# Chunked attention feeding a gated MLP on one core: the order of the SyncE queue, the staging of loads, and the casts of the opening

## The chip, the core and the metric

One NeuronCore of a Trainium2 chip. The time of a run is the device time of the program in microseconds. The kernels were run on several chips, so each is compared only with runs of the kernel before on the same chip. A run within 1.5% of the fastest of its kernel counts as fast.

## The reference, cut to what matters

```python
# q, k, v: 8 batches, 8 heads, 576 tokens, 64 columns; chunks of 64 tokens
scores = scale * np.matmul(q_c, k_c.transpose(0, 1, 2, 4, 3))
attn = softmax(scores)
x = np.matmul(attn, v_c) ...            # as 4608 tokens x 512
h = x @ w_in                            # 512 -> 2048
g = h * (1.0 / (1.0 + np.exp(-beta * h)))
out = g @ w_out                         # 2048 -> 512
```

Nearly all the arithmetic is in the two products with w_in and w_out. Attention is within chunks of 64 tokens and small.

## The kernel before

The tokens go through in nine blocks of 512: block b is the first 512 tokens of batch b, and block 8 collects the last 64 of each batch. For each block TensorE runs mm1 (x by w_in, 64 matmuls of 128x512, read from xT) and mm2 (g by w_out, 64 matmuls); the attention of the *next* block (scores, exp, attend, normalize) is strewn into mm2. So TensorE has always work, if the next block's xT is there when mm2 ends.

xT is x turned so that the 512 columns stand on partitions. From block 1 on this is done by DMA transposes; q and k are turned likewise from block 2 on (block 0 and 1 turn q and k on TensorE). All these transposes and all loads are issued by one engine, SyncE, in the order in which they stand; it waits for the data of the first in the queue before it looks at the second (a wait of 18.1 us of this kind is shown below). Stores are issued by ScalarE.

```python
def load(blk, name, m):                       # a quarter of q, k or v: 256 KB
    ...
    P.dma("sp", lambda e: e.dma_start(stage[name][r:r + n, 512 * m:512 * m + 512]..., drams[name]...),
          writes=[K(name + "stage", m, r, v=blk)])

def turn_qk(blk, name):                       # cast q or k of a whole block, turned
    P.dma("sp", lambda e: e.dma_start_transpose(turned[name]..., cast[name][:, :]), ...)

def turn_x(blk, m):                           # a quarter of x, turned
    P.dma("sp", lambda e: e.dma_start_transpose(xT[:, blk % 2, :, 128 * m:...], x_sb[:, m, :]), ...)
```

Every operation is given a time in an ideal schedule of 32 units a block, and `at(time, ...)` sorts them; this order is the order of each engine's queue. T is the moment at which mm2 of the block before starts.

```python
def attention(blk, T):
    # scores at T + 0.6, exp at T + 1 ...
    for u in range(2):
        for m in (2 * u, 2 * u + 1):
            at(T + 4.6 + 4 * u, attend, blk, m)
            at(T + 4.7 + 4 * u, normalize, blk, m)
            at(T + 4.8 + 4 * u, turn_x, blk, m)

def prepare(blk, T):
    for i, name in enumerate("qkv"):
        for m in range(4):
            at(T - 27 + 4 * i + m, load, blk, name, m)
            if name == "v":
                at(T - 8 + m, cast_v, blk, m, "pool")
            else:
                at(T - 14 + 4 * i + m, cast_qk, blk, name, m, "pool")
                if m == 3:
                    at(T - 10 + 4 * i, turn_qk, blk, name)
```

A block is 32 units, so the load of q for the next block, at T - 27, is at T + 5 of this one: between the turns of x at T + 4.8 and at T + 8.8. The loads have one staging buffer for each of q, k and v, and in the opening w_out is loaded into the staging of w_in:

```python
wstage = sb("wstage", [128, 4, 2048], F32)      # w_in pieces, then w_out pieces, in the same four slots
stage = {n: sb(n + "stage", [128, 2048], F32) for n in "qkv"}
...
at(-87.9, load_beta)      # the load on SyncE, and the halving of beta on VectorE right behind it
at(-80 + u, cast_qk4, 0, "q", u, "dve")         # later in VectorE's queue than beta
at(-0.5, cast_w_in, 1, 1, ("dve",))             # frees a slot of wstage
at(0, load_w_out, 0)
```

The softmax here doesn't subtract the row's maximum and nothing guards it: scores larger than these inputs give would overflow.

## Time and profile before

| what | kernel before |
|---|---|
| time | 358.55 us (median of 4, 355.67 to 360.55) |
| span of the profiled run | 354.5 us |
| TensorE busy | 293.9 us, 83% of the span |
| mm1 waits for xT | 25.1 us in 6 waits, and 4.3 more put down to "issue" |
| mm1 of block 1 starts at | 77.67 us |

The lines of the profile name the engines PE (TensorE's matmuls), PEld (its weight loads), DVE (VectorE), ACT (ScalarE), POOL (GpSimd), SP (SyncE) and SPq (SyncE's DMA queue); L399 is line 399 of the kernel, out<-in are the tiles written and read, and a bracket at the end of a line is the idle time before it in us, with what ended it. The clock is the share of full speed that was granted to TensorE.

These rows of the page give the busy share of TensorE and of the DMA engines in 40 slices of 8.9 us each, in tenths:

```profile
PE   0047998729996999799979995999499959999995
DMA  7980999998059946993899199908992499732013
```

TensorE has a dip (6, 7, 7, 5, 4, 5) about once in each four slices: the block boundaries. The DMA row has a 0 at the fourth slice, which the window of that stretch shows closer (length, busy time and count of PE, PEld, DVE, ACT, POOL, then clock, DMA share, GB/s), and SyncE's own waits give what the queue stood at:

```profile
26.30:35.40 9.10, 6.35 (x139) 5.05 (x140) 6.08 (x12) 3.70 (x7) 1.04 (x1) 1.00 0.01 2
```

```profile
SPq L267 <- DVE w_in_bf L259: 22.0, 3, 18.1
```

L267 is the load of w_out; it waited 22.0 us in three waits, the longest 18.1, for VectorE to empty the shared slots. And the copy of a turned k of block 0, on the timeline (start, us, engine, line, what):

```profile
25.15 2.43 DVE L259 COPY kT<-F 128x1024 bf16<-128x1024 bf16 x1 [1.38 <-PE F L327]
```

### The profile page before, as it was taken

How to read it: one execution, taken by the hardware profiler on the slowest of the kernel's cores; microseconds unless marked ns; L12 is line 12 of the kernel's file. 1: busy time of each engine (PE TensorE's matmuls, PEld its weight loads, DVE VectorE, ACT ScalarE, POOL GpSimd, SP SyncE). 2: the span in 40 equal slices, each digit the busy share in tenths (PEclk: the TensorE clock that was granted, in tenths of full speed). 3: DMA queues.
4: the chain of work that ended last, by engine and by line, in shares of the span. 5: the costliest groups of instructions: out<-in, count | busy, mean ns of one | idle time of the engine just before them, and what ended most of it. 6: DMA issues, size and time to landing. Idle time of an engine off the chain costs nothing.

```text
span 354.5 us, 5695 instructions
## 1 busy us (share of the span) xinstructions
PE 293.9 (83%) x2384; PEld 137.9 (39%) x2384; DVE 149.6 (42%) x237; ACT 153.5 (43%) x228; POOL 73.6 (21%) x112
## 2 busy tenths in 40 slices
PE   0047998729996999799979995999499959999995
PEld 0035444304442444244424441444144424444442
DVE  0166896306630653074317410743066306633810
ACT  1053777206711771176127512761167116715721
POOL 2321447411003400340034013300340024100000
PEclk9999999958998999899989996999789989999999
DMA  7980999998059946993899199908992499732013
GB/s 248 252 329 2 305 399 212 226 226 118 2 124 243 198 92 143 250 199 64 179 251 208 46 199 212 213 2 182 216 217 41 124 213 183 134 100 79 0 39 82
DMA packets 156665, 58.06 MB, mean 164 GB/s; under 512 B 144352, under 2 KB 149472, under 8 KB 156640
## 3 DMA queue, kind: packets, MB, share of 16 engines
q1 hardware_dynamic: 151392, 48.26, 66.3%
q10 hardware_dynamic: 5248, 9.44, 9.1%
q8 instruction: 19, 0.31, 0.4%
q14 instruction: 6, 0.05, 0.1%
HBM read 36.71 MB, written 9.44 MB: 130 GB/s over the span
## 4 chain that ended last, share of the span: by engine, by line
PE 62%; SPq 17%; DMA 9%; DVE 8%; issue 2%; ACT 1%
PE F L399 39%; PE F L414 18%; SPq L283 10%; DMA xT<-x_sb 8%; SPq L381 6%; DVE x_sb L375 3%; DVE kT L259 3%; PE A L348 2%; PE A L365 2%; DMA beta_raw<-in_moe_beta_dram 1%; PE F L327 1%; DVE qcast L259 1%; DVE rden L373 1%; SPq L311 1%; PE F L389 1%
## 5 line engine op out<-in xcount | busy, mean ns | idle before, releaser
L399 PE MATMUL F<-xT,w_in_bf 128*128 128x512 bf16 x576 | 139.8, 408 | 29.9 <-DMA xT<-x_sb 25.1
L407 DVE SCALAR_TENSOR_TENSOR g<-tt,F 128x512 bf16<-128x512 bf16 x144 | 98.5, 687 | 111.9 <-ACT tt L404 111.6
L414 PE MATMUL F<-w_out_bf,g 128*128 128x512 bf16 x576 | 130.3, 379 | 0.0
L404 ACT ACTIVATE tt<-F,beta_half 128x512 bf16<-128x512 f32 x144 | 99.0, 687 | 71.8 <-PE F L399 71.8
L399 PEld LDWEIGHTS F<-xT,w_in_bf 128*128 128x128 bf16 x576 | 59.1, 104 | 110.2 <-issue 51.1
L414 PEld LDWEIGHTS F<-w_out_bf,g 128*128 128x128 bf16 x576 | 54.3, 98 | 62.8
L419 ACT ACTIVATE ostage<-F 128x512 f32<-128x512 f32 x36 | 21.5, 597 | 93.9 <-PE F L414 93.9
L259 POOL CAST qcast<-qstage 128x512 bf16<-128x512 f32 x28 | 17.2, 614 | 134.1 <-DMA qstage<-in_q_dram 134.1
L373 DVE RECIPROCAL rden<-A 128x8 f32<-128x8 f32 x36 | 7.3, 203 | 55.2 <-PE A L365 55.2
L259 POOL CAST vaug<-vstage 128x512 bf16<-128x512 f32 x36 | 22.3, 619 | 35.8 <-DMA vstage<-in_v_dram 35.8
L259 POOL CAST kcast<-kstage 128x512 bf16<-128x512 f32 (+1 forms) x31 | 20.3, 655 | 35.7 <-DMA kstage<-in_k_dram 35.7
L375 DVE TENSOR_TENSOR x_sb<-A,rden 128x512 bf16<-128x512 f32 x36 | 24.9, 692 | 1.2
L354 ACT ACTIVATE E<-A 128x512 bf16<-128x512 f32 x36 | 18.7, 602 | 7.0 <-PE A L348 7.0
L327 PE MATMUL F<-identity,qcast 128*128 128x128 bf16 x16 | 2.0, 308 | 21.4 <-DVE qcast L259 21.4
L365 PEld LDWEIGHTS A<-vaug,E 64*64 64x64 bf16 x576 | 11.7, 112 | 8.4 <-issue 4.3
L365 PE MATMUL A<-vaug,E 64*64 64x65 bf16 x576 | 14.2, 198 | 0.9 <-ACT E L354 0.4
L256 ACT ACTIVATE qT<-F 128x1024 bf16<-128x1024 bf16 x2 | 4.9, 2442 | 19.6 <-PE F L327 19.6
L261 POOL TENSOR_SCALAR w_out_bf<-wstage 128x512 bf16<-128x512 f32 (+1 forms) x5 | 9.5, 1910 | 15.2 <-DMA wstage<-in_moe_w_out_dram 15.2
L348 PE MATMUL A<-qT,kT 64*64 64x64 bf16 x576 | 7.4, 199 | 4.0 <-DVE kT L259 3.9
L327 PEld LDWEIGHTS F<-identity,qcast 128*128 128x128 bf16 x16 | 1.5, 138 | 21.6 <-POOL w_in_bf L259 18.0
L348 PEld LDWEIGHTS A<-qT,kT 64*64 64x64 bf16 x576 | 6.1, 112 | 7.9 <-DVE kT L259 4.6
L228 DVE TENSOR_SCALAR beta_half<-beta_raw 128x16 f32<-128x16 f32 x1 | 0.9, 893 | 16.4 <-DMA beta_raw<-in_moe_beta_dram 16.4
(29 smaller groups left out, 48.2 us busy)
## 6 DMA issues: line engine op xcount, KB each, us to landing
vstage<-in_v_dram SPq DMA_DIRECT2D x32, 256.0 KB, 5.2
out_dram<-ostage ACTq DMA_DIRECT2D x32, 256.0 KB, 2.9
qstage<-in_q_dram SPq DMA_DIRECT2D x24, 256.0 KB, 5.1
kstage<-in_k_dram SPq DMA_DIRECT2D x24, 256.0 KB, 5.2
wstage<-in_moe_w_out_dram SPq DMA_DIRECT2D x4, 1024.0 KB, 10.5
wstage<-in_moe_w_in_dram SPq DMA_DIRECT2D x3, 1024.0 KB, 9.5
qstage<-in_q_dram SPq DMA_DIRECT2D x4, 512.0 KB, 6.1
kstage<-in_k_dram SPq DMA_DIRECT2D x4, 512.0 KB, 7.2
```

Of the source, the lines that this page charges most:

```text
L259: P.op(eng, lambda e: e.tensor_copy(dst, src), reads=r, writes=wr)
L283: return e.dma_start(stage[name][r:r + n, 512 * m:512 * m + 512].rearrange("p (h d) -> p h d", d=64), drams[name][b, :, t:t + n, :].rearra ...
L348: return e.matmul(A[64 * c2:64 * c2 + 64, bank, col:col + 64], turned["k"][r, hp, t], turned["q"][r, hp, t])
L354: P.op("act", lambda e: e.activation(E[:, bank, :], A[:, bank, :], AF.Exp, scale=0.125), reads=[K("A", bank, v=("s", blk))], writes=[K("E" ...
L365: return e.matmul(A[r, bank, 128 * (h % 4):128 * (h % 4) + 65], E[r, 2 * (m // 2) + h % 2, col:col + 64], vaug[r, m, h, 0:65])
L375: P.op("dve", lambda e: e.tensor_tensor(x_sb[:, m, :].rearrange("p (b h d) -> p b h d", h=4, b=2), o[:, :, :, 0:64], rden[:, m, :, :].unsq ...
L381: P.dma("sp", lambda e: e.dma_start_transpose(xT[:, blk % 2, :, 128 * m:128 * m + 128], x_sb[:, m, :]), reads=[K("x", m, v=blk)], writes=[ ...
L399: P.op("pe", lambda e, c=c: e.matmul(F[:, bank, :], w_in_bf[:, c, 256 * e0 + i:256 * e0 + 256:2], xT[:, blk % 2, c, :], start=(c == 0), st ...
L404: P.op("act", lambda e: e.activation(tt[:, T % NTT, :], F[:, bank, :], AF.Tanh, scale=beta_half[:, e0, i:i + 1]), reads=[K("F", bank, v=(" ...
L407: P.op("dve", lambda e: e.scalar_tensor_tensor(g2[:, t, :], tt[:, T % NTT, :], 1.0, F[:, bank, :], ALU.add, ALU.mult), reads=[K("F", bank, ...
L414: P.op("pe", lambda e, t=t: e.matmul(F[:, s, :], g2[:, t, 128 * s:128 * s + 128], w_out_bf[:, t, :], start=(t == 0), stop=(t == NT - 1)), ...
L419: P.op("act", lambda e: e.activation(ostage[:, N % NOS, :], F[:, s, :], AF.Copy), reads=[K("F", s, v=("o", N))], writes=[K("o", N % NOS, v ...
```

## The change

The intent has four parts. (1) Loads of blocks 3 to 8 stand so early that they run two blocks ahead, in doubled staging; in the SyncE queue of a period the four turns of x and the turns of the next q and k come first, the twelve loads last. (2) In the opening, q and k of block 0 are cast as they land, beta is halved later and by GpSimd. (3) w_out has its own staging, so its load waits for nothing. (4) Smaller things: turned q and k are written contiguously and read strided; x of block 1 is turned on TensorE; mm1 of block 0 starts with half the columns; three output stages instead of four, for room. The core of the diff:

```diff
-        wstage = sb("wstage", [128, 4, 2048], F32)
-        stage = {n: sb(n + "stage", [128, 2048], F32) for n in "qkv"}
+        wstage = sb("wstage", [128, 8, 2048], F32)
+        stages = {n: sb(n + "stage", [128, 2, 2048], F32) for n in "qkv"}
-        NOS = 4
+        NOS = 3
 ... (beta)
-            P.op("dve", lambda e: e.tensor_single_scalar(
+        def halve_beta():
+            P.op("pool", lambda e: e.tensor_single_scalar(
 ... (copies of turned q, k)
-            copy(eng, turned[name]....rearrange("x h (p i) -> x h i p", i=4),
-                 mid.rearrange("x (h i p) -> x h i p", h=2, i=4),
+            copy(eng, turned[name]....rearrange("x h (p i) -> x h p i", i=4),
+                 mid.rearrange("x (h i p) -> x h p i", h=2, i=4),
 ... (prepare)
-                    at(T - 27 + 4 * i + m, load, blk, name, m)
+                    at((T - 48 if blk > 3 else T - 42 if blk == 3 else T - 26) + 4 * i + m,
+                       load, blk, name, m)
                     if name == "v":
-                        at(T - 8 + m, cast_v, blk, m, "pool")
+                        at(T - (17 if blk > 2 else 9) + m, cast_v, blk, m, "pool")
                     else:
-                        at(T - 14 + 4 * i + m, cast_qk, blk, name, m, "pool")
+                        at(T - (41 if blk > 3 else 35 if blk == 3 else 22) + 4 * i + m,
+                           cast_qk, blk, name, m, "pool")
                         if m == 3:
-                            at(T - 10 + 4 * i, turn_qk, blk, name)
+                            at(T - (20 if blk > 2 else 12.5) + 2 * i, turn_qk, blk, name)
 ... (opening)
-            at(-80 + u, cast_qk4, 0, "q", u, "dve")
-            at(-80 + u, cast_qk4, 0, "k", u, "pool" if u == 0 else "dve")
-        at(0, load_w_out, 0)
-            at(4 * j + 0.6, load_w_out, j)
-            at(14, load, 1, "v", m)
+        at(-83, load_w_out, 0)
+            at(-61, load_w_out, j)
+            at(-60, load, 1, "v", m)
+            at(-79 + i, cast_qk4, 0, name, u, "dve")
+        at(-75, halve_beta)
 ... (x of block 1)
-                at(28.9 + 2 * u, turn_x, 1, m)
+            at(30.2 + 0.2 * m, turn_x_pe, 1, m, A, (0, 2, 1, 3)[m], ("act", "dve")[m % 2])
 ... (mm1 of block 0: columns 0 to 255 of its first four tiles first)
```

## The prediction

> **What bounds the kernel now.** I read the chain that ended last first, then the same chain in order of time, then windows, and at last the opening on a timeline. The chain by share, and the costliest group:
>
> ```profile
> PE 62%; SPq 17%; DMA 9%; DVE 8%; issue 2%; ACT 1%
> ...
> L399 PE MATMUL F<-xT,w_in_bf 128*128 128x512 bf16 x576 | 139.8, 408 | 29.9 <-DMA xT<-x_sb 25.1
> ```
>
> TensorE carries only 62% of the chain; 17% is time of SyncE's DMA queue (SPq) and 9% the flight of a transfer. The matmuls of the first product (mm1, L399) stood idle 29.9 us, nearly all for xT, the attention output turned by a DMA. In order of time, one block boundary (start us, us, what):
>
> ```profile
> 135.26 0.70 DVE x_sb L375
> ...
> 136.37 1.26 SPq L381
> ...
> 137.68 0.58 SPq L283
> 138.31 0.67 SPq L283
> 139.02 1.23 SPq L283
> 140.29 1.07 SPq L283
> ...
> 141.42 1.84 SPq L381
> ...
> 143.31 3.53 DMA xT<-x_sb
> ...
> 146.98 15.66 PE F L399 x64
> ```
>
> L283 is the load of q, k or v; L381 the turn of x. Four q loads of the next block stand in the queue between the second and the third turn of x, although x was ready: 3.7 us of issuing, and then the last turn flies 3.53 us behind loads. Windows (length, then busy time by engine, PEclk, DMA share, GB/s), the first two over a whole period of 128 matmuls of 512 columns, the second two over mm1 just after a wait and later:
>
> ```profile
> 128.67:162.64 33.97, 31.72 (x258) 14.43 (x256) 14.43 (x25) 15.45 (x24) 7.25 (x12) 0.95 0.82 171
> ...
> 306.61:336.60 29.99, 29.94 (x257) 14.08 (x256) 14.41 (x25) 15.45 (x24) 0.00 (x0) 1.00 0.19 55
> ...
> 146.90:150.70 3.80, 3.72 (x10) 0.55 1.15 269
> 150.70:162.60 11.90, 11.90 (x57) 1.00 0.98 193
> ```
>
> The last period has no loads behind it, and it is the model for the change: 29.99 us, TensorE busy for 29.94. The others take 34.73, 33.97, 33.95, 37.01, 37.39 and 35.62 us by the starts in the chain. Part is the wait, and part that after the wait the clock is at 0.55 for 3.8 us, which makes mm1 15.66 instead of 13.81 us.
>
> Opening, on the timeline:
>
> ```profile
> 14.46 0.61 POOL L259 CAST vaug<-vstage 128x512 bf16<-128x512 f32 x1 [0.42 <-DMA vstage<-in_v_dram]
> ...
> 16.37 0.89 DVE L228 TENSOR_SCALAR beta_half<-beta_raw 128x16 f32<-128x16 f32 x1 [16.37 <-DMA beta_raw<-in_moe_beta_dram]
> 17.17 0.68 DVE L259 CAST qcast<-qstage 128x1024 bf16<-128x1024 f32 x1
> ```
>
> VectorE does nothing until beta lands at 16.37, because halving beta stands first in its queue. By the landings of the issues, q and k of block 0 were there at 4.7, 6.2, 8.1 and 9.8 us. Meanwhile the DMA, with 7 MB delivered by 26 us, has nothing to do from 26.3 to 35.4 us (2 GB/s in that window): w_out shares w_in's staging and waits for its last cast (SPq L267 waited 22.0 us for VectorE's w_in casts).
>
> [...] Here the copies of turned q and k took 2.43 us for 1024 columns, 2.4 ns each, with a destination step of 8 bytes. [...]
>
> **The change, part by part.** Work on TensorE does not fall. It moves orders, staging and waits.
>
> *Steady state, blocks 3 to 8.* The queue becomes: four turns of x, turn of next q and k, then twelve loads for the block after. I place a period from the start of mm2. The x tiles are ready at about +6.5, +7.3, +10.7 and +11.5 us (135.1 to 140.2 less 128.67). The last turn is issued by about +13.3 (318.97 plus 1.25 in the quiet last boundary, less 306.61). q and k's turns take 3.6 and 1.4 us of issuing, to about +18.5. Twelve loads took 3.68, 4.58 and 5.64 = 13.9 us, so to +32.4, which is +2.4 of the next period, before x is ready there at +6.5. So no load stands before a turn of x, with about 4 us of slack. Predicted period 30.0, plus 0.3 residual. The five periods that hold the boundaries of blocks 3 to 7 cost 33.97 + 33.95 + 37.01 + 37.39 + 35.62 = 177.9; five at 30.3 are 151.5: 26.4 us saved.
>
> *Block 2 boundary.* Its turns stand behind block 3's loads, which cannot be issued much earlier since q and k of block 2 must be loaded, cast and turned first. v of block 1 should be in at 48 us (below), q, k, v of block 2 at 64 to 66, their turns issued until 69, so loads of block 3 until about 83 and the four turns until 88; landed about 91 to 92. mm1 could have started at about 86.5. I estimate 5 us of wait, 1.9 us of half clock after it (15.66 less 13.81) and 0.7 before scores for k's turn: 7.6 us. Before, this period lost 34.73 - 29.99 = 4.7. So 2.9 us worse.
>
> *Opening.* The last k tile lands at 9.8, is cast (0.68), turned on TensorE (1.1) and copied out ([...]2.43 now): about 13.5 us instead of 27.58. Before, 7.2 us lie between that and mm1 (scores, exp, attend, normalise, turn); half of the columns may start after two tiles, so about 6.4: mm1 starts at 20 instead of 34.8. Its weights follow: w_in pieces landed at 16.1, 17.9, 21.5, 24.2 and 26.8, each before its turn comes in 14 us of mm1. mm1 ends at about 34.5 instead of 48.84. The DMA goes on at the measured 370 to 390 GB/s for large rows: w_out's first MB at 29.5, q and k of block 1 at 35, the rest of w_out at 43, and v at 48 (1.2 us per 256 KB). mm2 of block 0 with the attention of block 1 takes 20.2 us in the trace of before (48.84 to 69.08), partly waiting for copies; v's casts and PE turns allow its end at about 55. mm1 of block 1 then starts at 55.5 instead of 77.67: 22.2 us saved. In this the turn on TensorE replaces a queue wait of 8.6 us and adds about 1 us of transposes. With no long gap, mm1 of block 1 also keeps its clock (16.27 against 13.82): 2.4 us.
>
> *Sum:* -26.4 - 22.2 - 2.4 + 2.9 = -48.1; span 354.5 - 48.1 = 306.4 us. Timed runs had a median 5.0 above the profiled span, the profiled execution itself 1.7; I add 3.5: 310 us.
>
> *What costs nothing:* GpSimd takes beta and more casts, but is busy 21% of the span. Three instead of four output stages: stores leave every 3.5 to 4.2 us and land in 2.9, so three suffice.
>
> **The rivals.** (a) The DMA becomes the bound. The periods have a DMA share of 0.82 to 0.87 of 34 to 37 us, 28 to 32 us of packet time, no less than the new period of 30. For it: v loads of 256 B packets get only 210 to 220 GB/s. Against it: the share reaches 1.3 to 1.5 in slices, so packets overlap and their time includes waiting; and from 127.8 to 133.8 it is nearly idle. If true, periods of 32 to 33 and about 325 us. (b) A residual wait stays at each boundary: the last turn issued at about +12 lands at +15 to +17.5, and mm2 ends at about +16.2. With landings of 3.5 to 5 instead of 2.4 to 2.8 us, 1 to 2 us are left in each of five periods: 312 to 320. Speaking against it: the last boundary of before had four output stores beside it and no wait. (c) The opening is bound by DMA or by VectorE (20.84 busy of 22.60 from 35.4 on), so that block 1 starts at 60 and not 55.5: 315. (d) Block 2 goes well, as its loads come sooner than I think: 303.
>
> **Range and chances.** (b), (c) and (d) move the sum by -7 to +10, (a) by +15 at small odds. I predict 310, and 302 to 322 for 8 in 10. To stay within 2%, nearly all of both savings would have to fail: faster 0.97, same 0.02, slower 0.01.
>
> **What would show it.** In the profile of the changed kernel: VectorE's first cast at about 5 us; mm1 of block 0 at about 20, of block 1 at about 55 us; no idle DMA slice in the first 60 us; mm1's mean falling from 408 to near 380 ns and its idle time to under 10 us, most of it at block 2; SPq in the chain down to a few per cent and PE over 85%; periods of 30 from block 3 on; copies to qT and kT under 2 us. I am wrong if xT waits appear at every boundary, if block 1 still starts after 62, or if periods sit at 32 and more with the DMA share at its ceiling.

## The result, and the profile after

The changed kernel took **308.64 us** (median of 4, 307.36 to 310.04) against 358.55. The ratio is 0.8614, with a 95% interval from 0.8539 to 0.8689. Ratios here are formed from the fast runs of both kernels in the same rounds, so they are not quite the quotient of the medians that stand beside them. The profiled span is 306.4 us, TensorE 92% busy. All outputs are right.

The rows of the page, now with slices of 7.7 us:

```profile
PE   2489999999949999999999999999999999999994
DMA  7999999999999965999599959996999970340022
```

The dips at the boundaries are gone but one, in slice 12. The DMA row has no idle slice until slice 34, some 250 us in.

Where the time came from is best seen in mm1's lines on the timeline, block by block, as each line has the length of mm1 and, in brackets, how long TensorE sat idle before it and for what. Before, blocks 1, 2, 4, 6 and 8 (start, us):

```profile
77.67 16.27 PE L399 MATMUL F<-xT,w_in_bf 128*128 128x512 bf16 x64 [8.59 <-DMA xT<-x_sb]
113.01 15.66 PE L399 MATMUL F<-xT,w_in_bf 128*128 128x512 bf16 x64 [3.01 <-DMA xT<-x_sb]
...
180.93 15.66 PE L399 MATMUL F<-xT,w_in_bf 128*128 128x512 bf16 x64 [2.23 <-DMA xT<-x_sb]
...
254.28 16.71 PE L399 MATMUL F<-xT,w_in_bf 128*128 128x512 bf16 x64 [4.62 <-DMA xT<-x_sb]
...
322.62 13.98 PE L399 MATMUL F<-xT,w_in_bf 128*128 128x512 bf16 x64
```

After, blocks 1, 2, 3 and 8 (a record is missing from each group, hence x63):

```profile
57.77 13.97 PE L402 MATMUL F<-xT,w_in_bf 128*128 128x512 bf16 x63 [0.31 <-ACT xT L258]
91.67 15.66 PE L402 MATMUL F<-xT,w_in_bf 128*128 128x512 bf16 x63 [3.87 <-DMA xT<-x_sb]
123.75 13.97 PE L402 MATMUL F<-xT,w_in_bf 128*128 128x512 bf16 x63 [0.37 <-DMA xT<-x_sb]
...
274.51 13.98 PE L402 MATMUL F<-xT,w_in_bf 128*128 128x512 bf16 x63
```

Two things change together: the wait goes, and with it the slow clock that came after it (16.71 us after a wait of 4.62, against 13.97 for the same 64 matmuls without one). With "period" for the time from one end of mm1 to the next, the whole span is accounted for:

| step | before | after | difference |
|---|---|---|---|
| mm1 of block 1 starts | 77.67 | 57.77 | -19.9 |
| length of that mm1 | 16.27 | 13.97 | -2.3 |
| period of block 2 | 34.73 | 35.59 | +0.9 |
| periods of blocks 3 to 7 | 177.94 | 151.29 | -26.65 |
| period of block 8 | 29.99 | 29.87 | -0.1 |
| rest (mm2 of block 8, last store) | 17.9 | 17.9 | 0 |
| span | 354.5 | 306.4 | -48.1 |

In blocks 3 to 7 the waits before mm1 went from 2.25 + 2.23 + 4.40 + 4.62 + 4.31 = 17.81 us to 0.37 + 0.19 + 0 + 0.60 + 0 = 1.16, and the five mm1 from 79.83 to 69.86 us in all. That is 16.65 of wait and 9.97 of clock, together 26.62 of the 26.65: six tenths of the steady gain are waits and four tenths the clock after them.

The SyncE queue over one period shows how (start, us of issuing, what; L384 is the turn of x, L300 that of q or k, L285 a load):

```profile
117.99 3.13 SPq L384 DMA_TRANSPOSE xT<-x_sb  x2
121.16 2.17 SPq L300 DMA_TRANSPOSE qT<-qcast  x1
123.38 2.85 SPq L300 DMA_TRANSPOSE kT<-kcast  x1
126.67 4.25 SPq L285 DMA_DIRECT2D qstage<-in_q_dram  x4
130.97 4.84 SPq L285 DMA_DIRECT2D kstage<-in_k_dram  x4
135.85 4.71 SPq L285 DMA_DIRECT2D vstage<-in_v_dram  x4
144.19 5.95 SPq L384 DMA_TRANSPOSE xT<-x_sb  x3
```

The loads end at 140.56, and the queue stands free for 3.6 us before x comes at 144.19. The chain at that boundary, in order of time, has no load between the turns any more:

```profile
149.20 0.94 SPq L384
...
150.18 3.66 DMA xT<-x_sb
...
153.98 5.77 PE F L402 x26
```

The last turn still flies 3.66 us, but TensorE, at work on mm2 until then, sat idle for only 0.19 us before this mm1. Windows over the periods of blocks 2, 3 and 4 (the last three columns are clock, DMA share and GB/s):

```profile
71.74:107.33 35.59, 31.40 (x254) 14.42 (x256) 14.41 (x25) 15.45 (x24) 12.11 (x20) 0.95 1.17 218
107.33:137.72 30.39, 29.71 (x253) 14.02 (x256) 14.41 (x25) 15.45 (x24) 5.71 (x10) 1.00 0.94 174
137.72:167.95 30.23, 29.72 (x254) 13.97 (x256) 14.41 (x25) 15.45 (x24) 7.62 (x13) 1.00 1.03 195
```

From block 3 on TensorE is busy 29.7 of 30.3 us at a clock of 1.00. A DMA share of 0.94 and 1.03 in these two periods did not slow them. Block 2 is the exception, and the queue before it tells why:

```profile
77.36 5.01 SPq L285 DMA_DIRECT2D vstage<-in_v_dram  x4
82.42 7.31 SPq L384 DMA_TRANSPOSE xT<-x_sb  x4
```

The turns of block 2's x begin at 82.42, at once behind the loads of block 3, and end at 89.73.

The opening: VectorE's first cast is at 4.68, beta is halved on GpSimd at 18.70 (0.26 us), and mm1 of block 0 starts at 21.23 instead of 34.80:

```profile
4.68 0.69 DVE L261 CAST qcast<-qstage 128x1024 bf16<-128x1024 f32 x1 [4.68 <-DMA qstage<-in_q_dram]
...
13.40 1.23 DVE L261 COPY kT<-F 128x1024 bf16<-128x1024 bf16 x1 [1.13 <-PE F L329]
```

### The profile page after: what moved, and what is told of

It reads as the page before. It is cut to its first block, busy times and chain, and to the rows that moved or that the text cites. A ratio compares the mean times of both kernels' runs of the same rounds, so it can differ in the third digit from the quotient of the medians.

```text
span 306.4 us, 5766 instructions
## 1 busy us (share of the span) xinstructions
PE 281.6 (92%) x2380; PEld 137.4 (45%) x2416; DVE 144.4 (47%) x238; ACT 148.6 (49%) x230; POOL 75.7 (25%) x115
## 4 chain that ended last, share of the span: by engine, by line
PE 62%; DMA 14%; SPq 13%; DVE 6%; issue 2%; ACT 1%; POOL 1%; POOLq 0%
PE F L421 28%; PE F L402 28%; DMA kstage<-in_k_dram 5%; SPq L285 5%; DMA qstage<-in_q_dram 4%; SPq L384 4%; SPq L300 3%; DMA xT<-x_sb 3%; PE A L368 3%; DVE x_sb L378 3%; DMA vstage<-in_v_dram 2%; PE A L352 1%; DVE rden L376 1%; DVE kT L261 1%; PE A L329 1%
## 5 line engine op out<-in xcount | busy, mean ns | idle before, releaser
L402 PE MATMUL F<-xT,w_in_bf 128*128 128x512 bf16 (+1 forms) x583 | 128.7, 380 | 6.5 <-DMA xT<-x_sb 5.0
L421 PE MATMUL F<-w_out_bf,g 128*128 128x512 bf16 x549 | 127.3, 379 | 2.4 <-issue 1.0
L411 ACT ACTIVATE tt<-F,beta_half 128x512 bf16<-128x512 f32 x144 | 98.6, 687 | 37.5 <-PE F L402 37.5
L402 PEld LDWEIGHTS F<-xT,w_in_bf 128*128 128x128 bf16 x592 | 58.2, 100 | 76.3 <-issue 9.8
L261 POOL CAST vaug<-vstage 128x512 bf16<-128x512 f32 x36 | 21.6, 616 | 48.4 <-PE A L368 27.9
L261 POOL CAST kcast<-kstage 128x512 bf16<-128x512 f32 (+1 forms) x30 | 19.5, 651 | 21.8 <-DMA kstage<-in_k_dram 21.8
L263 POOL TENSOR_SCALAR w_out_bf<-wstage 128x512 bf16<-128x512 f32 x7 | 11.4, 1645 | 3.1 <-DMA wstage<-in_moe_w_out_dram 3.1
L261 POOL CAST w_in_bf<-wstage 128x1024 bf16<-128x1024 f32 x5 | 5.2, 1041 | 7.4 <-DMA wstage<-in_moe_w_in_dram 7.4
L261 DVE CAST qcast<-qstage 128x1024 bf16<-128x1024 f32 x4 | 3.1, 792 | 7.7 <-DMA qstage<-in_q_dram 7.7
L258 ACT ACTIVATE qT<-F 128x1024 bf16<-128x1024 bf16 x2 | 2.0, 1024 | 8.4 <-PE F L329 8.4
```

The lines of the kernel that those rows point to most:

```text
L261: P.op(eng, lambda e: e.tensor_copy(dst, src), reads=r, writes=wr)
L402: P.op("pe", lambda e, c=c: e.matmul(F[:, bank, lo:hi], w_in_bf[:, c, 256 * e0 + i:256 * e0 + 256:2], xT[:, blk % 2, c, lo:hi], start=(c = ...
L411: P.op("act", lambda e: e.activation(tt[:, T % NTT, :], F[:, bank, :], AF.Tanh, scale=beta_half[:, e0, i:i + 1]), reads=[K("F", bank, v=(" ...
L421: P.op("pe", lambda e, t=t: e.matmul(F[:, s, :], g2[:, t, 128 * s:128 * s + 128], w_out_bf[:, t, :], start=(t == 0), stop=(t == NT - 1)), ...
```

## The experiments

The theory before the runs: the steady gain comes from the order of the SyncE queue; the opening's gain from casts that no longer stand behind beta; and block 2 pays back part of the latter, because its turns stand behind block 3's loads. The rivals: the steady gain comes from loading two blocks ahead into second buffers; the opening's gain from w_out's own staging or the cheaper copies; and nothing is paid back at block 2.

| run | what | us (lowest to highest) | ratio to before, 95% interval |
|---|---|---|---|
| e1 | after, but the old queue order from block 3 | 341.01 (339.58 to 342.13) | 0.9532 [0.9460, 0.9604] |
| e2 | x turns first, but loads one block ahead, before q and k turns | 345.68 (344.36 to 346.59) | 0.9673 [0.9595, 0.9752] |
| e3 | two ahead, but q and k turns behind the loads | 341.51 (340.32 to 345.03) | 0.9565 [0.9479, 0.9651] |
| e4 | beta halved first on VectorE again | 313.49 (313.41 to 313.98) | 0.8768 [0.8710, 0.8826] |
| e5 | w_out in the staging of w_in | 310.29 (309.30 to 311.09) | 0.8651 [0.8600, 0.8701] |
| e6 | strided writes of turned q and k again | 306.31 (305.88 to 307.02) | 0.8543 [0.8495, 0.8591] |
| e7 | x of block 2 turned on TensorE | 300.22 (299.84 to 300.72) | 0.8376 [0.8321, 0.8431] |
| e8 | v of block 3 loaded after block 2's turns | 303.73 (302.14 to 304.57) | 0.8464 [0.8410, 0.8518] |
| e9 | the changed kernel again, as control | 308.00 (306.72 to 308.73) | 0.8594 [0.8552, 0.8636] |
| e10 | e7, and block 2's casts a little later | 300.28 (298.92 to 301.04) | 0.8371 [0.8330, 0.8411] |
| e11 | one block ahead; loads of v behind q and k turns | 308.96 (308.56 to 310.00) | 0.8620 [0.8561, 0.8678] |
| e12 | e11 with a single staging buffer for each of q, k, v | 308.03 (307.54 to 308.43) | 0.8597 [0.8535, 0.8660] |

Each is the median of four runs, of six for e9 and e10. The kernel before had medians of 358.1 (e1 to e4), 359.46 (e5 to e8), 359.49 (e9 to e11) and 358.56 (e12) beside them.

### The queue from block 3 on: e1, e2, e3

**e1** keeps everything of the change but gives blocks 3 to 8 the old order.

```diff
-   at((T - 48 if blk > 3 else T - 42 if blk == 3 else T - 26) + 4 * i + m, load, blk, name, m)
+   at(T - (27 if blk > 2 else 26) + 4 * i + m, load, blk, name, m)
    # cast_v at T - 8, cast_qk at T - 14 and turn_qk at T - 10 + 4 * i, as before, for blk > 2
```

> The changed kernel with the queue order of before from block 3 on: loads one block ahead, q loads between the two pairs of turns of x, k and v loads before the turns of q and k. The opening stays changed. My theory (the place in the SyncE queue makes the boundary waits): the six periods of blocks 2 to 7 go back to 34 to 37 us as in before, 212.7 in all instead of 186.9, so about 332 us span and 334 us timed. Rival (the waits of before came from the late opening, or shrink once the opening is early): periods stay near 30 to 31, and under 315 us.

Measured: 341.01 us. The cause is confirmed, the size was expected too small. mm1 of block 1 starts at 56.46, so the opening is kept whole, but the periods from block 2 to 7 are 37.56, 37.44, 37.54, 34.82, 37.12 and 37.52 us. The waits came back, longer than before, and with them a slower mm1 (timeline, block 2):

```profile
91.18 16.81 PE L402 MATMUL F<-xT,w_in_bf 128*128 128x512 bf16 x63 [4.69 <-DMA xT<-x_sb]
```

So on the changed opening, the queue order of blocks 3 to 8, with the lead of two blocks that e1 takes back as well, is worth about 33 us (0.9532 less 0.8614, of 358), and the rest of the change about 17 (358.1 less 341.0). Why the old order costs 37.5 us here and 34 to 37 in the kernel before was not settled: the four q loads between the turns took 5.12 us to issue instead of 3.7.

**e2** puts the turns of x first, but loads only one block ahead, and all twelve loads stand before the turns of q and k.

```diff
-   at((T - 48 if blk > 3 else T - 42 if blk == 3 else T - 26) + 4 * i + m, load, blk, name, m)
+   at(T - (23 if blk > 2 else 26) + 4 * i + m, load, blk, name, m)
    # casts and turn_qk as in e1
```

> Only the order changed from the old queue: the four turns of x stand first, then the loads of the next block, one block ahead, then its q and k turns. My theory: x no longer waits, but the turn of k is issued 32 us after the start of mm2 and lands about 4 us after the next mm2 has begun, so the scores wait some 3 us in each of six periods (33 to 34 us), while block 2's boundary no longer waits: about 321 us. Rival (order alone is the gain, two blocks ahead adds nothing): 301 to 306 us.

Measured: 345.68 us, slower than e1. Both expectations missed, and this was the most instructive run. The wait moved from xT to the scores, which wait for kT. SyncE's queue, and TensorE's two lots of scores around it:

```profile
112.92 7.21 SPq L384 DMA_TRANSPOSE xT<-x_sb  x4
120.17 3.25 SPq L285 DMA_DIRECT2D qstage<-in_q_dram  x4
123.47 5.28 SPq L285 DMA_DIRECT2D kstage<-in_k_dram  x4
128.79 4.71 SPq L285 DMA_DIRECT2D vstage<-in_v_dram  x4
133.54 3.68 SPq L300 DMA_TRANSPOSE qT<-qcast  x1
137.26 1.47 SPq L300 DMA_TRANSPOSE kT<-kcast  x1
```

```profile
105.61 0.76 PE L352 MATMUL A<-qT,kT 64*64 64x64 bf16 x64 [4.47 <-DMA kT<-kcast]
141.94 1.07 PE L352 MATMUL A<-qT,kT 64*64 64x64 bf16 x64 [4.63 <-DMA kT<-kcast]
```

This is a loop. From the scores of one block to the first turn of its x: 7.3 us. Four turns of x: 7.2. Twelve loads of the next block: 13.4. Turns of its q and k: 5.2. Flight until the scores of the next block: 3.2. The sum is 36.3 us, and 141.94 - 105.61 is 36.33. Every member waits for the one before, so TensorE can be no faster than this loop, although its own work is under 30 us a period.

**e3** keeps the loads two blocks ahead, but puts the turns of q and k behind them.

```diff
-   at(T - (20 if blk > 2 else 12.5) + 2 * i, turn_qk, blk, name)
+   at(T - (4.2 if blk > 2 else 12.5) + 2 * i, turn_qk, blk, name)
    # and cast_qk at T - 33 instead of T - 41 for blk > 3
```

> Loads two blocks ahead as in the change, but the turns of the next q and k stand behind the twelve loads of the block after. My theory: k's turn lands about 4 us after the next mm2 starts and the scores wait about 3 us in each of six periods, with block 2's boundary as in the change: about 326 us. Rival (the turn of q and k has slack anyway): within 2 us of 308.

Measured: 341.51 us, 15 us more than expected. The waits of the whole run (us, times, longest):

```profile
PE A L352 <- DMA kT<-kcast: 25.0, 5, 7.7
```

The same loop stands again, although the loads in it are now of another block and the second buffers are in use. In the period from the scores at 144.35 to those at 181.60 us its parts are 8.0 (scores to the first turn of x), 7.3 (turns of x), 13.7 (loads), 5.7 (turns of q and k) and 2.6 (flight): 37.25 us. So loading ahead did not help here, with the turn that the next step needs issued behind the loads: 341.51 us against the 308.64 of the changed kernel.

### Is it two blocks ahead, or the length of the loop: e11 and e12

If the loop is right, one block ahead should do, provided that the loads of v, which no turn waits for, leave it. 36.3 less 4.7 is under 32. For this the casts of q and k move forward too, so that their turns can stand before the loads of v; the two moves were not run apart.

```diff
    # against e2, for blk > 2:
-   at(T - 14 + 4 * i + m, cast_qk, blk, name, m, "pool")
-   at(T - 10 + 4 * i, turn_qk, blk, name)
+   at(T - 22.9 + 4 * i + m, cast_qk, blk, name, m, "pool")
+   at(T - 15.5 + 0.2 * i, turn_qk, blk, name)        # v is loaded from T - 15 on
```

> Loads one block ahead, queue order x turns, q and k loads, q and k turns, v loads. My theory after the last runs: with one block ahead the queue is a loop (scores, x, loads, turn of k, next scores) and its length sets the period; taking the four v loads (4.7 us) and the cast of v out of it brings the turn of k to land at about the start of the next scores, so periods of 30 to 32 us and no block 2 wait: 304 to 316 us. Rival (two blocks ahead is needed, what costs is loads in flight beside the turns): 330 us and more.

Measured: 308.96 us, against 345.68 for e2 and 308.00 for the control. The queue and the scores:

```profile
116.11 3.26 SPq L285 DMA_DIRECT2D qstage<-in_q_dram  x4
119.42 5.23 SPq L285 DMA_DIRECT2D kstage<-in_k_dram  x4
124.69 3.64 SPq L300 DMA_TRANSPOSE qT<-qcast  x1
129.20 1.86 SPq L300 DMA_TRANSPOSE kT<-kcast  x1
131.11 3.71 SPq L285 DMA_DIRECT2D vstage<-in_v_dram  x4
```

```profile
103.14 0.73 PE L352 MATMUL A<-qT,kT 64*64 64x64 bf16 x64 [0.98 <-DMA kT<-kcast]
133.68 0.73 PE L352 MATMUL A<-qT,kT 64*64 64x64 bf16 x64 [0.44 <-DMA kT<-kcast]
```

The loop is now 30.54 us, about as long as TensorE's own work of 29.9, and the wait before these scores is under 1 us. The casts on GpSimd are now a part of it: the turns of q and k waited 25.1 us for them after the opening, in 12 waits of at most 3.4. The period of block 8, whose loads are twice as many pieces of 64 rows, was 34.58 and not 29.9 us; it eats what this order gained at block 2 (30.04 instead of 35.59). Then the buffers:

```diff
-   stages = {n: sb(n + "stage", [128, 2, 2048], F32) for n in "qkv"}
+   stages = {n: sb(n + "stage", [128, 1, 2048], F32) for n in "qkv"}      # and index 0 instead of blk % 2
```

> The order of the run before (x turns, q and k loads, their turns, v loads, one block ahead) with one staging buffer each for q, k and v, as the kernel before had them. My theory: nothing ever waits for the second buffer in that order, the casts of a block being done 15 us before the next loads: 308 to 311 us, as with two. Rival (the second buffer is needed, loads wait for casts): 315 us and more.

Measured: 308.03 us; no different from e11 or the control. After the first 60 us its loads waited 1.1 us in all for casts. The second staging buffers of q, k and v are one way to break the loop, not what the gain needs.

### The opening: e4, e5, e6

**e4** gives halving beta back its place at the head of VectorE's queue.

```diff
-            P.op("pool", lambda e: e.tensor_single_scalar(beta_half, ...
+            P.op("dve", lambda e: e.tensor_single_scalar(beta_half, ...
-        at(-75, halve_beta)
+        at(-87.85, halve_beta)
```

> The changed kernel with beta halved first on VectorE, as before. The first mm1 then starts about 10 us later (31.5 instead of 21.2 us). My theory: the block 2 boundary is tied to the DMA stream, which does not move, so its 3.9 us wait and 1.8 us of slow clock vanish, and only about 4 us are left: 312 us. Rival (the savings add up, each boundary moves with TensorE): 10 us slower, 318 us.

Measured: 313.49 us, as the theory said. mm1 of block 0 starts at 31.2 and of block 1 at 67.86, 10.1 us later than in the changed kernel, yet the span is only 5.3 us longer (311.7 against 306.4). The timeline has the other half, for blocks 1 and 2:

```profile
67.86 13.97 PE L402 MATMUL F<-xT,w_in_bf 128*128 128x512 bf16 x63 [0.30 <-ACT xT L258]
98.16 13.97 PE L402 MATMUL F<-xT,w_in_bf 128*128 128x512 bf16 x63 [0.27 <-DMA xT<-x_sb]
```

mm1 of block 2 no longer waits and keeps its clock. So about half of the 10 us that this part brings is given back at block 2, whose xT is tied to the DMA stream and does not come earlier because TensorE does: the loads that stand before its turns end at 82.4 us in the changed kernel and at 82.0 in e4, with TensorE 10.1 us later.

**e5** loads w_out into the slots of w_in again, in the same place in the queue.

```diff
-                return e.dma_start(wstage[:, 4 + j, :]..., a)
+                return e.dma_start(wstage[:, j, :]..., a)
    # load_w_out(0) at -74, the others at 4 * j - 3.4 (1 later for j = 1), v of block 1 at 9
```

> The changed kernel with w_out staged in w_in's four slots again, the order of the queue unchanged, so that the w_out loads wait for w_in's casts. My theory: with beta out of the way the casts come early (17.7 to 29.8 us on GpSimd and VectorE), while the queue is backed up with loads, so the wait costs no idle DMA: within 1 us of 308.6. Rival (the 9 us of idle DMA of before came from the shared staging): 4 to 9 us slower, 313 to 318.

Measured: 310.29 us (309.30 to 311.09), against 308.00 (306.72 to 308.73) for the control, on the same chip: about 2 us slower, a little more than the theory allowed and far less than the rival. They were run at other times. The intervals of the ratios overlap, but no run of e5 is as fast as the slowest of the control, and mm1 of block 2 waited 4.80 us for xT and that of block 3 1.38, where in the control they waited 4.01 and not at all. SyncE waited 4.8 us for the slots, 2.8 at the longest, where in the kernel before it had waited 22.0 and 18.1: once the casts of w_in come early (in the changed kernel from 17.69 to 29.77 us; in the kernel before VectorE's four began at 34.7 to 44.3), the slots are free early. Own staging is worth about 2 us; the long wait of before, and the idle DMA with it, were the fault of the late casts.

**e6** writes the turned q and k strided again.

```diff
-   copy(eng, turned[name]....rearrange("x h (p i) -> x h p i", i=4), mid.rearrange("x (h i p) -> x h p i", ...
+   copy(eng, turned[name]....rearrange("x h (p i) -> x h i p", i=4), mid.rearrange("x (h i p) -> x h i p", ...
```

> The changed kernel with the copies of turned q and k writing in steps of 8 bytes again (2.43 instead of 1.02 and 1.23 us). My theory: the first mm1 starts about 2.4 us later and mm2 of block 0 another 2 us, but block 2's wait, tied to the DMA stream, shrinks by as much: within 1.5 us of 308.6. Rival (the savings add up): 3 to 5 us slower, 312 to 314.

Measured: 306.31 us, if anything below the control (and 2.3 below the 308.6 of the expectation, which allowed 1.5). The copies cost their 1.2 us more each, and mm1 of block 1 starts at 59.66, but mm1 of block 2 starts when it started anyway:

```profile
90.82 13.97 PE L402 MATMUL F<-xT,w_in_bf 128*128 128x512 bf16 x63 [1.13 <-DMA xT<-x_sb]
```

It started at 91.67 and 90.39 in the two profiles of the changed kernel. What the copies take is taken from the wait at block 2; and after this wait, of 1.13 us, mm1 took 13.97 us and not the 15.66 that it took after 3.87 and 4.01 in the changed kernel's two profiles. The cheaper copies save nothing while that deadline stands. Whether e6 is really a little faster is open: its highest run is above the control's lowest.

### Block 2, and a kernel that beats both: e7, e8, e10

**e7** takes block 2's x off the queue: it is turned on TensorE, as that of block 1.

```diff
+                    if blk == 2:
+                        at(T + 10.2 + 0.2 * m, turn_x_pe, 2, m, A, (0, 2, 1, 3)[m], ("act", "dve")[m % 2])
+                    else:
                         at(T + 4.8 + 4 * u, turn_x, blk, m)
```

> The changed kernel with the x of block 2 turned on TensorE instead of by the DMA. My theory: the 3.9 us wait before mm1 of block 2 and the 1.8 us of slow clock after it vanish, at about 1 us of transposes: 4 to 5 us faster, 304 us. Rival (something else ends there, for instance the turns of q and k of block 2 or the loads): within 1 us of 308.6.

Measured: 300.22 us, more than expected: block 2's period is 30.77, and those of blocks 3 to 6 are 29.87 to 29.88 (block 7's is 30.38), against 30.2 to 30.6. The queue, with four turns less, is ahead: it comes to the turn of block 3's q at 81.07 us instead of 89.77. That this lead is what removes the last tenths of the later periods fits, but was not tested by itself.

```profile
86.53 13.98 PE L402 MATMUL F<-xT,w_in_bf 128*128 128x512 bf16 x62
```

**e8** leaves the turns on the queue and moves four loads instead.

```diff
-   T - 42 if blk == 3
+   (T - 25.9 if name == "v" else T - 42) if blk == 3
```

> The changed kernel with v of block 3 loaded after the turns of x of block 2, so that the first two turns do not stand behind it. My theory: the last turn lands 3 to 4 us sooner, the wait before mm1 of block 2 falls from 3.9 us to under 1 and the clock stays up: 4 to 5 us faster, 304 us. Rival (the turns are slow because the DMA is backed up with loads, not because of their place): at most 2 us faster.

Measured: 303.73 us, as expected; mm1 of block 2 starts at 87.98 behind 1.40 us of idle time, a little more than expected, which the profile puts down to a copy of ScalarE and no longer to xT, and takes 13.97. Block 3 now waits 1.48 us for its xT. Two different ways of freeing the queue remove the same wait, and e8 moves as many loads as before, only later: so it was the place of block 3's loads, ahead of those turns.

**e9** is the changed kernel once more, on the chip of e10 and e11.

> The changed kernel itself, as the control for the two beside it: 308.6 us again, 306 to 311, with 35 to 36 us for the period of block 2 and 30 for those after it.

Measured: 308.00 us; the result stands, and mm1 of block 1 started at 56.4 this time, so 1.4 us of that start vary between executions.

**e10** is e7 with the casts of block 2's q and k a little later, so that the casts of block 1's v come first on GpSimd.

```diff
-   T - (41 if blk > 3 else 35 if blk == 3 else 22) + 4 * i + m, cast_qk
+   T - (41 if blk > 3 else 35 if blk == 3 else 21.6) + 4 * i + m, cast_qk
```

> x of block 2 turned on TensorE, and GpSimd casts v of block 1 before the first q of block 2. My theory: the first half alone gave 300.2; the second removes the wait for v's cast in mm2 of block 0 (0.4 us on TensorE): 299 to 300 us. Rival (the opening is set by the DMA stream, which the order of casts does not touch): no different from 300.2.

Measured: 300.28 us, no different from e7. Either beats both kernels: 16% below the kernel before and 2.5% below the changed one. TensorE is busy 94% of e10's span, and mm1's group waits 1.2 us in all.

## Why the prediction was right

The time was predicted at 310 and measured at 308.64; the sum of the steps, -48.1 on the span, met the measured -48.1 to the tenth. That is partly luck, since two terms erred in opposite directions: the opening gave 2.3 us less than forecast, and block 2 cost 2.0 less.

- *Steady state, -26.4*: measured -26.65, by the mechanism told. No load stands before a turn of x, the periods are 30.2 to 30.6 in blocks 3 to 6, and e1 takes the gain away by undoing the order, and with it the lead. The queue is free 3.6 us before x comes; "about 4 us of slack" had been read off the old trace.
- *Opening, -22.2*: measured -19.9 in this profile (-21.3 in the control's, whose mm1 of block 1 starts at 56.35). Half of it is beta (e4). The last copy of k ended at 14.6 and not 13.5; mm1 of block 0 started at 21.2 instead of 20 and ended near 37.5 instead of 34.5, partly since its first 32 half-width matmuls took 4.89 us, where 16 full ones take 3.5 (a quarter of 13.97). The copies were put under 2 us, the author's estimate, which no trace had shown; they took 1.23 on VectorE and 1.02 on ScalarE. That did not matter, as e6 shows.
- *Clock of mm1 of block 1, -2.4*: measured -2.3.
- *Block 2, +2.9*: measured +0.9. The wait was 3.87 and not 5, the clock cost 1.69 and not 1.85, and the wait of 0.7 before the scores did not appear. e7 and e8 show the mechanism. But the step stood for more than the prediction made of it: e4 and e6 show that block 2's start is a deadline set by the DMA, so that the last microseconds of any earlier opening are lost there.
- *Rival (a), the DMA as the bound*: fell. The periods of 30.2 to 30.4 us have a share of 0.94 to 1.03 while TensorE is busy 29.7 us of them, so a share of about 1 was no ceiling for the period. *Rival (b), a residue at each boundary*: 1.16 us in five boundaries and not 1 to 2 in each. The slow landings that it feared came, though: the last turn flew 3.6 to 3.9 us in blocks 3 to 6, and at block 4 it landed at 153.84, 0.14 us before mm1 started, so the boundary has nothing to spare. *Rival (c), the opening*: block 1 started at 57.77 here and at 55.8 to 57.3 in seven more runs with the same opening, between the 55.5 of the sum and the 60 of the rival. *Rival (d), block 2 going well*: its wait was 1.1 us shorter than forecast, but it stayed.
- *Readings that were off, with little effect on the sum*. 318.97 + 1.25 - 306.61 is 13.6 and not 13.3. At the boundary shown, x was not ready all the time that the four q loads took: its third quarter was written at 139.30 us, so they held it up for 2.1 of their 3.7 us. The last turn's flight of 3.53 us was put down to the loads ahead of it; in the changed kernel, with no load issued for 9 us before it, it flew 3.66, so that flight is no evidence for this (the third turn's does fit: 4.9 us behind the q loads, 2.9 without). And 15.66 is a length, 13.81 a time from start to start; the length at full clock is 13.97.
- *A check that failed*: "SPq in the chain down to a few per cent and PE over 85%". The chain of the changed kernel is

```profile
PE 62%; DMA 14%; SPq 13%; DVE 6%; issue 2%; ACT 1%; POOL 1%; POOLq 0%
```

though mm1's group says that nothing waited much:

```profile
L402 PE MATMUL F<-xT,w_in_bf 128*128 128x512 bf16 (+1 forms) x583 | 128.7, 380 | 6.5 <-DMA xT<-x_sb 5.0
```

The chain follows each step back to what released it last, also over a gap of 0.16 us, and then runs for 20 us along loads and GpSimd casts that cost nothing. With the waits this small its shares no longer say what bounds the kernel; the idle time before the groups does. (mm1's 6.5 us and mean of 380 ns were as predicted: under 10, near 380.)

What the prediction had not seen is in the experiments, not in the sum. It took the two-block lead and the doubled staging as part of what makes the steady state work. e12 shows neither is needed, and e2 and e3 show a loop through the scores that the prediction did not name, and which the expectations for e1 to e3 therefore undersized. It also named w_out's shared staging as the cause of the idle DMA; e5 shows that the late casts were, and that sharing costs about 2 us once they are early.

Left open: the other half of the opening. In e4, with beta in its old place, mm1 of block 1 still starts 9.8 us earlier than in the kernel before (67.86 against 77.67). Most of that must be the wait of 8.59 us that went when x of block 1 was turned on TensorE, but no run took this back by itself (e7 shows the same move for block 2), nor the half-width start of mm1. Open also: what three output stages instead of four cost (a fourth did not fit beside the doubled staging, so it was not run), and what the new queue would bring on the old opening.

## What to carry to other kernels

Where one queue issues the turns, loads and stores of a block, look for the loop (result, its turn, the loads behind it, the turn that the next result needs) and add up its issue times and flights: its length set the period here, 36.3 us in e2 and 30.5 in e11, with the same bytes moved. Put what the next step waits for ahead of loads that nobody waits for yet, and take off the loop whatever no turn needs; a longer lead or more buffers gained nothing here where they did not shorten it (e3 with both took 341.51 us, e12 with neither 308.03). And when one stage is made earlier, ask which later start is tied to something else, for there the gain is given back (about 5 of 10 us in e4), unless, as with block 2 here, that tie is cut too.

## What these traces show of the clock, the issue times and the copies

- The clock after a wait: after waits of 2.23 to 4.11 us mm1 took 15.66 instead of 13.97 us, and after waits of up to 1.54 us it kept its 13.97. In e3 the scores behind a wait of 2.72 us took 0.73 us and the 15 matmuls of mm2 after them 3.40, while behind a wait of 4.53 us they took 1.07 and 5.25. The slowing does not simply grow with the wait: mm1 took 16.55 to 16.93 us after 4.38 to 4.77, but 15.25 after 4.31, 15.27 after 4.80 (e5) and 16.27 after 8.59. In the kernel before, the seven mm1 that followed a wait took 111.8 us instead of 97.8: 14.0 us, or 3.9% of the span, about half as much again as the waits themselves (29.4 us).
- The time that SyncE's queue takes to issue a DMA: beside the 5 to 6 us from issue to landing (medians of 4.9 to 5.7 for loads of 256 KB) one issue is short, but in one queue these times add up. A load of 256 KB in 256-byte rows holds SyncE's queue for 0.8 to 1.3 us (e2: 3.25 for four of q, 5.28 for four of k, 4.71 for four of v). For the DMA transposes of this kernel it is about 1.8 us for 128x512 of x (7.21 for four) and 1.5 to 3.7 us for 128x2048 of q or k (e2: 1.47 and 3.68). Together they kept the queue for some 26 of 30 us of a period (7.2 + 5.0 + 13.8).
- Strided copies of bf16 from PSUM on VectorE: with the source stepping 256 bytes 1.23 us for 1024 columns, 1.2 ns each; with the destination stepping 8 bytes 2.43 us, 2.4 ns each.
